# The last stage's first matrix product with seven half products for eight in 5 of 16 blocks

## The chip, the cores and the metric

One Trainium2 chip; the kernel runs on one of its cores, in one launch. The metric is the device time of that launch in microseconds. Before the change it is 961.84 us, the median of three runs (960.94 to 963.04).

## What is computed

Attention over 4 x 12 heads of 448 tokens, a routed mixture of 8 experts with two products each, and a last stage of two products with an ELU between them, on 1792 tokens. The last stage is what is changed:

```
def _moe2_ref(x, w_in, w_out):              # x 1792 x 768, w_in 768 x 2048, w_out 2048 x 768
    h = x @ w_in
    g = np.where(h > 0.0, h, np.exp(np.minimum(h, 0.0)) - 1.0)
    return g @ w_out
```

The products are made in float16 pairs: a number is a high half plus a low half, and a product takes three matmuls (high x high, high x low, low x high).

## The kernel before

Attention and routing fill some 300 us, the experts (e = 0 to 7, lines L974 and L1011) the time to 546 us, then come layer 1 (L1090) and layer 2 (L1137) of the last stage. All engines work from queues of instructions in order; which order they have is settled when the program is built, by a scheduler that simulates the engines.

The tokens stand in `xc` as two halves h of 896 columns, cut into block 0 (512 columns of either half) and block 1 (384). Layer 1 runs over f = 0 to 7. For each f it takes the columns f and f + 8 of `w_in` (r = 0, 1; 128 columns each) and makes four tiles (h, r) for block 0 and four for block 1, each of 6 x 3 = 18 matmuls into one PSUM bank (tags `b` and `c`, three banks each). `wi_prep(f + 1)` runs at f: it loads two tiles of `w_in` in float64 words, three integer steps on VectorE make float32 of each (L854 to L856), ScalarE makes the high half (L919) and VectorE the low one (L920). `wo_prep` does the same for the second matrix (L1024 to L1031), with the sums that layer 2 needs.

After each tile comes the ELU in three steps: ScalarE's Exp of PSUM (L1092), VectorE's clamp `min(e, 1) - 1` in place (L1093), and VectorE's maximum of that and the PSUM tile (L1094). The tile `e` (five buffers) is then stored to `g_d` in DRAM (L1098). Layer 2 loads it from there (`q`, L1050), and makes sums of it and splits them (L1057 to L1067).

Layer 2 already makes seven half products for eight, with the function `winograd`: 2 x 2 blocks of tokens and weights, four sums of the tokens' blocks (S1 to S4), four of the weights' (T1 to T4), and products accumulated over three PSUM banks a, b and c. `product` issues the matmuls, `snap` copies a bank to SBUF, `add` adds a bank to such a copy, `copy` takes a bank as it is. Its sums T1 and T3 of the weights come back from DRAM to the tile `ex` (L1039), T4 to `xc` after layer 1 is through with it.

GpSimd makes the low halves `xh` of the experts' gathered rows (L938; the last at 475.59 us), and then stands idle until layer 2's scattered stores (L1153).

Of the kernel before, what the change touches and what calls it, by code (L numbers as in the profile page):

```python
# [5 lines left out]
F32 = mybir.dt.float32  # L6
F16 = mybir.dt.float16
# [13 lines left out]
P = 128  # L21
# [748 lines left out]
CH2 = 1.0 / (SO * SW * SW * SY * SW)  # L770
COUT = 1.0 / (SG * SW)

# [10 lines left out]
class Weights:  # L783
# [28 lines left out]
    def fetch(self, pool, w2_d):  # L812

        self.f2 = [pool.tile([P, 1024], F32, name=f"b{d}") for d in range(6)]
        self.w2 = []
        for f, x in zip(self.f2, w2_d[0]):
            self.nc.sync.dma_start(f, x)
# [45 lines left out]


PS = ("a", 2), ("b", 3), ("c", 3)
A11, A12, S2, S3, S1, S4, A22 = range(7)
# [34 lines left out]

def moe(tc, xp, pre, xs, idx, idh, W, rows, ring, w1_d, w2_d, wi_d, wo_d, lin, g_d, t_d, out):
    nc = tc.nc
    with tc.tile_pool(name="mp", bufs=1, space=PSUM, reuse_waits="tile") as pp:
# [6 lines left out]

        wic = {}

        def wi_prep(f):

            for f in (f, f + 8):
                a = W.read64(wi_d[f], f"wi{f}")
                w = wic[f] = ring.tile([P, 2, 768], F16, tag="w1", name=f"wic{f}", bufs=8)
                nc.scalar.activation(w[:, 0], a, AF.Copy, scale=SW)  # L919
                nc.vector.scalar_tensor_tensor(w[:, 1], a, SW, w[:, 0], ALU.mult, ALU.subtract)  # L920

        words = ExitStack()
        W.stage64 = words.enter_context(tc.tile_pool(name="w64", bufs=1, side="right", reuse_waits="tile"))
        with tc.tile_pool(name="m1", bufs=1, reuse_waits="tile") as sp:
# [5 lines left out]
            def columns(e):  # L930
# [3 lines left out]
                for h in (1, 0):  # L934
                    for a in range(0, DM, n):
                        x32, hi, lo = xg[h][0:112, a:a + n], hl[h][0:112, 0, a:a + n], hl[h][0:112, 1, a:a + n]
                        nc.scalar.activation(hi, x32, AF.Copy)  # L937
                        (nc.vector if e == 0 else nc.gpsimd).tensor_tensor(lo, x32, hi, ALU.subtract)  # L938
                xe[e] = x
# [9 lines left out]
            def result(e, d, ps):  # L949

                ps = ps.rearrange("p (h c) -> p h c", h=2)
                for c, (a, b) in zip(xc, CB):
                    lo, hi = max(a, 112 * e), min(b, 112 * e + 112)
                    if lo < hi:
                        z, c = ps[:, :, lo - 112 * e:hi - 112 * e], c[:, :, d, :, lo - a:hi - a]
                        nc.scalar.activation(c[:, :, 0], z, AF.Copy, scale=SY)
                        nc.vector.scalar_tensor_tensor(c[:, :, 1], z, SY, c[:, :, 0], ALU.mult, ALU.subtract)

            with tc.manual_schedule():
# [29 lines left out]
            for e in range(E):  # L989
# [16 lines left out]
                for d in range(6):  # L1006
# [5 lines left out]
                    result(e, d, ps)  # L1012
        pre.close()
        with tc.tile_pool(name="wb", bufs=1, reuse_waits="tile") as wp:
            WO = (0,), (1,), (2, 3), (4,), (5,), (6,), (7,), ()
            wb = wp.tile([P, 3, 8, 2, 384], F16, name="wb")


            ex = wp.tile([P, 14336], F16, name="ex")

# [58 lines left out]
            with tc.tile_pool(name="l1", bufs=1, side="right", reuse_waits="tile") as sp:  # L1079
                def layer1(f, cb, made=None):  # L1080

                    c0, c1 = CB[cb]
                    n = c1 - c0
                    for k, (h, r) in enumerate(((0, 0), (0, 1), (1, 0), (1, 1))):
                        t, bufs = PS[2 - k % 2]
                        ps = pp.tile([P, 512], F32, name=f"l{f}_{cb}{h}{r}", tag=t, bufs=bufs)[:, 0:n]
                        w = wic[f + 8 * r]
                        for d in range(6):
                            for m, (i, j) in enumerate(((0, 0), (0, 1), (1, 0))):
                                nc.tensor.matmul(ps, w[:, i, d * P:(d + 1) * P], xc[cb][:, h, d, j], start=d == 0 and m == 0, stop=d == 5 and m == 2)  # L1090
                        e = sp.tile([P, 512], F32, tag="e", name=f"e{f}_{cb}{h}{r}", bufs=5)[:, 0:n]
                        nc.scalar.activation(e, ps, AF.Exp, scale=CH2)  # L1092
                        nc.vector.tensor_scalar(e, e, 1.0, -1.0, ALU.min, ALU.add)  # L1093
                        nc.vector.scalar_tensor_tensor(e, ps, CH2, e, ALU.mult, ALU.max)  # L1094
                        if made is not None:
                            made[2 * r + h] = e
                        g = slice(c0 // P, c1 // P)
                        store = nc.sync.dma_start(g_d[g, 2 * r + h, :, f].rearrange("g p c -> p g c"), e.rearrange("p (g c) -> p g c", c=P))  # L1098
                    return store

                for f in range(8):
# [8 lines left out]
                    late = {}  # L1110
                    layer1(f, 0, late)
                    if f == 7:
                        first = operands(0, late)
                        next(first)
                        wt = {T3: load_t(T3, ex[:, 0:6144]), T1: load_t(T1, ex[:, 6144:12288])}
                    last = layer1(f, 1)
                wt |= {k: [wb[:, k, f] for f in range(8)] for k in (B11, B21, B22)}
# [51 lines left out]
def body(tc, i, out):  # L1169
    nc = tc.nc  # L1170
    with tc.tile_pool(name="lg", bufs=1) as lp, tc.tile_pool(name="ring", bufs=1, side="right") as ring, tc.tile_pool(name="dr", bufs=1, space=DRAM) as dp:
# [12 lines left out]
        with tc.tile_pool(name="xc", bufs=1, reuse_waits="tile") as xp:  # L1184
            pre = ExitStack()
            W.fetch(pre.enter_context(tc.tile_pool(name="pre", bufs=1, reuse_waits="tile")), i["w2"])
            rt.run(L, idx, row, W, rows.gather)
            moe(tc, xp, pre, xs, idx, idh, W, rows, ring, i["w1"], i["w2"], i["wi"], i["wo"], lin, g_d, t_d, out)

# [15 lines left out]
```

## Time and profile before

| | |
|---|---|
| median of three runs | 961.84 us |
| profiled execution | 961.21 us |
| its span in the trace | 959.4 us |
| mean granted TensorE clock | 0.997 |
| TensorE busy | 934.2 us (97%) |
| VectorE busy | 729.9 us (76%) |
| ScalarE busy | 524.8 us (55%) |
| GpSimd busy | 282.7 us (29%) |

Times in the trace run from the start of the span. Busy time is a mean over stages: VectorE's 76% are more than 95% in some stretches and half of that in others. In the rows, a name such as `e` stands for all its buffers; `out<-in` says what an instruction writes and reads. The idle time in a group's row is that of the engine just before its instructions, and the arrow names what ended it.

### The profile page before, as it was taken

Reading aid. Unit: us, or ns where it says so; the run is one execution under the profiler, and the core shown is the slowest. Engines: PE = TensorE matmul, PEld = TensorE weight load, DVE = VectorE, ACT = ScalarE, POOL = GpSimd, SP = SyncE. Lnnn points to the kernel's source line nnn. Section 1 sums busy time; section 2 is a strip of 40 time slices with the busy share of each in tenths; the row PEclk is TensorE's granted clock in tenths of the full one; section 3 lists DMA queues with packets and bytes.
Section 4 is the critical chain, followed back from the end, with each engine's and each line's share of the span. In section 5 each row is a group of like instructions: output and inputs, shape, how many; then the busy total and the mean of one; then the engine's idle time right before and its main releaser. Section 6 shows DMA issues by size and latency. Waiting matters only on the chain.

```text
span 959.4 us, 18741 instructions
## 1 busy us (share of the span) xinstructions
PE 934.2 (97%) x6927; PEld 620.7 (65%) x6927; DVE 729.9 (76%) x1433; ACT 524.8 (55%) x1147; POOL 282.7 (29%) x470
## 2 busy tenths in 40 slices
PE   7999999999987999999999999999999999999997
PEld 3555555555544899999999855555555566666664
DVE  8999998899867887777777799999825576555430
ACT  7989999999844666665664334333313333333320
POOL 5779999999423422221000000000000000000000
PEclk9999999999999999999999999999999999999999
DMA  9544444453254788776774377887763662332000
GB/s 349 201 136 121 139 122 153 120 168 79 56 166 158 182 293 268 245 239 215 241 213 142 132 259 237 267 269 252 229 204 105 173 231 92 119 101 99 33 33 33
DMA packets 100352, 164.93 MB, mean 172 GB/s; under 512 B 32672, under 2 KB 65952, under 8 KB 99872
## 3 DMA queue, kind: packets, MB, share of 16 engines
q1 hardware_dynamic: 96048, 152.66, 50.5%
q0 software_dynamic: 2400, 11.01, 3.4%
q8 instruction: 56, 0.92, 0.4%
q10 hardware_dynamic: 1808, 0.01, 0.2%
q14 instruction: 40, 0.33, 0.1%
HBM read 131.66 MB, written 31.99 MB: 171 GB/s over the span
## 4 chain that ended last, share of the span: by engine, by line
PE 87%; DVE 7%; DMA 2%; ACT 1%; issue 1%; POOL 0%; POOLq 0%; DVEq 0%; ACTq 0%
PE l L1090 23%; PE o_b L1137 11%; PE py L1011 10%; PE ph L974 10%; PE o L319 7%; PE o_c L1137 6%; PE s L242 5%; PE pt L295 5%; PE o_a L1137 3%; DMA fw<-w 1%; DVE w L843 1%; PE s L235 1%; PE pt L293 1%; DVE s L247 1%; PE pk L204 1%
## 5 line engine op out<-in xcount | busy, mean ns | idle before, releaser
L1090 PE MATMUL l<-xc,wic 128*128 128x384 f16 (+1 forms) x1152 | 218.2, 352 | 0.0
L1090 PEld LDWEIGHTS <-wic 128*128 128x128 f16 x1152 | 112.7, 98 | 104.9
L1137 PEld LDWEIGHTS <-a 128*128 128x128 f16 x1080 | 105.7, 98 | 69.8
L1153 POOL DMA_INDIRECT out<-xc,id x14 | 13.9, 992 | 463.6 <-issue 311.5
L843 DVE SCALAR_TENSOR_TENSOR w<-fw,w 128x768 f16<-128x768 f32 (+1 forms) x98 | 112.8, 1153 | 25.8 <-ACT w L841 25.8
L1011 PE MATMUL py<-h,w 128*128 128x224 f16 x1152 | 113.8, 259 | 1.5 <-DVE h L976 1.5
L1011 PEld LDWEIGHTS <-w 128*128 128x128 f16 x1152 | 109.9, 98 | 1.9 <-issue 1.6
L247 DVE TENSOR_REDUCE s<-s 128x1 f32<-128x448 f32 x168 | 104.7, 626 | 5.5 <-PE s L242 4.9
L266 ACT ACTIVATE p<-s,nb,r 128x448 f32<-128x448 f32 x144 | 104.4, 726 | 4.2 <-DVE nb L253 3.0
L974 PE MATMUL ph<-xe,w 128*128 128x224 f16 x1008 | 99.1, 259 | 1.5 <-DVE h L976 1.1
L974 PEld LDWEIGHTS <-w 128*128 128x128 f16 x1008 | 96.5, 98 | 1.8 <-issue 1.8
L841 ACT ACTIVATE w<-fw 128x768 f16<-128x768 f32 (+1 forms) x98 | 90.7, 928 | 5.5 <-DMA fw<-w 5.4
L1092 ACT ACTIVATE e<-l 128x512 f32<-128x512 f32 (+1 forms) x64 | 34.6, 540 | 103.7 <-PE l L1090 103.7
L304 ACT ACTIVATE e<-pt 128x448 f32<-128x448 f32 (+2 forms) x208 | 80.9, 429 | 14.5 <-PE pt L295 14.1
L319 PE MATMUL o<-e,v 128*64 128x448 f32 x384 | 87.8, 558 | 0.0
L295 PE MATMUL pt<-idn,p 128*128 128x128 f32 x432 | 70.9, 276 | 0.9 <-ACT p L266 0.9
L295 PEld LDWEIGHTS pt<-idn,p 128*128 128x128 f32 x432 | 50.0, 141 | 24.0 <-ACT e L304 12.3
L1067 DVE SCALAR_TENSOR_TENSOR a<-s,a 128x1024 f16<-128x1024 f32 (+2 forms) x30 | 33.4, 1116 | 39.1 <-ACT a L1066 39.1
L938 POOL TENSOR_TENSOR xh<-xg,xh 112x768 f16<-112x768 f32 x14 | 25.7, 1853 | 122.9 <-ACT xh L937 122.8
L242 PE MATMUL s<-ks,qh 128*128 128x448 f16 x144 | 51.2, 355 | 1.9 <-ACT p L266 1.0
L1137 PE MATMUL o_b<-wb,a 128*128 128x384 f16 x312 | 51.8, 326 | 0.0
L242 PE MATMUL s<-ks,ql 128*128 128x448 f16 x144 | 50.7, 352 | 0.0
(242 smaller groups left out, 1598.4 us busy)
## 6 DMA issues: line engine op xcount, KB each, us to landing
fw<-w SPq DMA_DIRECT2D x56, 384.0 KB, 3.8
fw<-w SPq DMA_DIRECT2D x42, 512.0 KB, 4.6
xwi<-wi SPq DMA_DIRECT2D x16, 768.0 KB, 7.4
xwo<-wo SPq DMA_DIRECT2D x16, 768.0 KB, 4.9
q<-g_d SPq DMA_DIRECT2D x24, 512.0 KB, 3.7
qT<-qT SPq DMA_DIRECT2D x24, 448.0 KB, 4.5
qk<-qk SPq DMA_DIRECT2D x23, 448.0 KB, 3.7
g_d<-e SPq DMA_DIRECT2D x32, 256.0 KB, 4.3
```

Of the source, the lines that this page charges most:

```text
L242: nc.tensor.matmul(ps[:, 0:448], q[:, o:o + P], ks[:, 448 * h:448 * h + 448], start=n == 0, stop=n == 1)
L247: nc.vector.tensor_reduce(d["s", u][:, 448:449], d["s", u][:, 0:448], AX.X, ALU.max, negate=True)
L266: nc.scalar.activation(dst, d["s", u][:, 0:448], AF.Exp, bias=d["nb", u], scale=d["r"][:, rc:rc + 1], accum_out=d["sm"][:, rc:rc + 1])
L295: nc.tensor.transpose(pt[:, j * P:(j + 1) * P], p[j][:, h, 64 * h + c * P:64 * h + (c + 1) * P], idn)
L304: move = nc.vector.tensor_copy if u in on else lambda o, x: nc.scalar.activation(o, x, AF.Copy)
L319: nc.tensor.matmul(d["o"][64 * h:64 * h + 64, 0:448], d["v"][:, c + 4 * h, :], d["e", min(2 * c + h, 6)], start=c == 0, stop=c == 3)
L841: nc.scalar.activation(w[:, 0], f, AF.Copy, scale=SW)
L843: nc.vector.scalar_tensor_tensor(w[:, 1], f, SW, w[:, 0], ALU.mult, ALU.subtract)
L974: mm = nc.tensor.matmul(ps, w[:, i, d * P:(d + 1) * P], x[:, d, j], start=d == 0 and n == 0, stop=d == 5 and n == 2)
L1011: nc.tensor.matmul(ps, w[:, i, f * P:(f + 1) * P], h[:, f, j], start=f == 0 and n == 0, stop=f == 7 and n == 2)
L1090: nc.tensor.matmul(ps, w[:, i, d * P:(d + 1) * P], xc[cb][:, h, d, j], start=d == 0 and m == 0, stop=d == 5 and m == 2)
L1137: nc.tensor.matmul(ps, a[x][:, f, i], wt[b][f][:, j], start=first and f == 0 and k == 0, stop=f == 7 and k == 2, skip_group_check=True)
```

## The change

For f = 2 to 6 block 0 is made by `winograd` (`fewer`), with the two halves of the tokens, the two halves of the 768 rows of `w_in` and the two column groups r as the 2 x 2 blocks: seven half products of 9 matmuls take the place of eight. Block 1 stays as it was (`plain`); its four tiles are issued between the half products, after A11, S2, S3 and A22. The four sums of the tokens' blocks are made by `combine` on GpSimd, in 12 rounds of 8 instructions (4 groups of 128 columns by 3 groups of 128 rows), queued behind the last instruction `xh`. The sums of the weights are made in `wi_prep` for these f: four sums and two more splits each. The tiles for the sums and for the copies (`kept`) share one place with `ex`, which is therefore free only after f = 6.

The ELU changes for all f: after Exp, ScalarE makes relu(1 - exp), and VectorE takes the minimum of that and -x. What is stored has its sign turned, and `COUT` turns it back.

Instructions in the order of the program are shown at three places. Names are tiles with their numbers; `sums` is the tile of the tokens' sums, `xc0` block 0.

GpSimd at the end of the experts, before:

```order
L898 DMA xg7_0_8981<-xs_63,idx_70 112x768
L938 TENSOR_TENSOR xh6_0_8986<-xg6_0_8527,xh6_0_8986 112x768
L938 TENSOR_TENSOR xh7_1_9425<-xg7_1_8982,xh7_1_9425 112x768
L938 TENSOR_TENSOR xh7_0_9424<-xg7_0_8981,xh7_0_9424 112x768
L1153 DMA out<-xc1_6525,id2_6526 1792x768 x14
```

and now:

```order
L953 TENSOR_TENSOR xh7_1_9421<-xg7_1_8978,xh7_1_9421 112x768
L953 TENSOR_TENSOR xh7_0_9420<-xg7_0_8977,xh7_0_9420 112x768
L983 TENSOR_TENSOR sums_6850<-xc0_6519 128x256 x3
L983 TENSOR_TENSOR sums_6850<-sums_6850 128x256
L983 TENSOR_TENSOR sums_6850<-sums_6850 128x128
L983 TENSOR_TENSOR sums_6850<-xc0_6519 128x256 x2
L983 TENSOR_TENSOR sums_6850<-sums_6850 128x128
L991 CAST sums_6850<-sums_6850 128x4x128
L983 TENSOR_TENSOR sums_6850<-sums_6850 128x4x128
L983 TENSOR_TENSOR sums_6850<-xc0_6519 128x256
```

Between the last `xh` and layer 2's stores (`out`) stand 96 instructions on `sums`.

VectorE near the second and third tile of f = 2, before (`wic`: split weights of layer 1, `awo`: words of the second matrix, `l2_001`: PSUM tile):

```order
L856 SCALAR_TENSOR_TENSOR awi4_10831<-xwi4_10832,awi4_10831 128x768
L1093 TENSOR_SCALAR e2_001_10682<-e2_001_10682 128x512
L856 SCALAR_TENSOR_TENSOR awi12_10840<-xwi12_10841,awi12_10840 128x768
L856 SCALAR_TENSOR_TENSOR awo4_10849<-xwo4_10850,awo4_10849 128x768
L1093 TENSOR_SCALAR e2_010_10706<-e2_010_10706 128x512
L1094 SCALAR_TENSOR_TENSOR e2_001_10682<-l2_001_10663,e2_001_10682 128x512
L920 SCALAR_TENSOR_TENSOR wic4_10837<-awi4_10831,wic4_10837 128x768
L1024 TENSOR_TENSOR t12_4_10861<-awo4_10849 128x384
L920 SCALAR_TENSOR_TENSOR wic12_10846<-awi12_10840,wic12_10846 128x768
L1094 SCALAR_TENSOR_TENSOR e2_010_10706<-l2_010_10687,e2_010_10706 128x512
```

and now, at the end of f = 2's block 0 (`l2_b` and `l2_c` are the banks b and c):

```order
L1122 SCALAR_TENSOR_TENSOR e2_110_10868<-l2_110_10849,e2_110_10868 128x384
L1161 SCALAR_TENSOR_TENSOR sums_6850<-l2_b_10755,sums_6850 128x512
L1067 SCALAR_TENSOR_TENSOR wb_10167<-awo4_10972,wb_10167 128x384
L855 TENSOR_SCALAR awo12_10978<-xwo12_10979 128x768
L921 SCALAR_TENSOR_TENSOR wic12_10957<-awi12_10948,wic12_10957 128x768
L933 TENSOR_TENSOR ti34_4_10961<-awi4_10942,ti12_4_10960 128x384
L1161 SCALAR_TENSOR_TENSOR sums_6850<-l2_c_10756,sums_6850 128x512
L921 SCALAR_TENSOR_TENSOR wic(4, 1)_10966<-ti12_4_10960,wic(4, 1)_10966 128x768
L856 SCALAR_TENSOR_TENSOR awo12_10978<-xwo12_10979,awo12_10978 128x768
L1122 SCALAR_TENSOR_TENSOR e2_011_10884<-sums_6850,e2_011_10884 128x512
L1122 SCALAR_TENSOR_TENSOR e2_111_10917<-l2_111_10898,e2_111_10917 128x384
L1122 SCALAR_TENSOR_TENSOR e2_010_10923<-sums_6850,e2_010_10923 128x512
```

The clamps (L1093) are gone, the sums of PSUM and copies (L1161) have come, and four splits `wic` stand for two.

SyncE's queue near the loads of `ex`, before:

```order
L1033 DMA t_d_67<-u12_7_11587 128x2x768
L1033 DMA t_d_67<-u34_7_11588 128x2x768
L1098 DMA g_d_66<-e5_000_11378 128x4x128
L1039 DMA ex_10077<-t_d_67 128x6144 x2
L1098 DMA g_d_66<-e5_001_11402 128x4x128
L1098 DMA g_d_66<-e5_010_11426 128x4x128
```

and now:

```order
L1124 DMA g_d_66<-e6_011_11868 128x4x128
L1124 DMA g_d_66<-e6_111_11901 128x3x128
L1124 DMA g_d_66<-e6_010_11907 128x4x128
L1075 DMA ex_12030<-t_d_67 128x6144 x2
L1124 DMA g_d_66<-e6_001_11921 128x4x128
L1124 DMA g_d_66<-e7_000_11953 128x4x128
L1124 DMA g_d_66<-e7_001_11977 128x4x128
L1086 DMA q0_2_12032<-g_d_66 128x896
L1086 DMA q0_1_12033<-g_d_66 128x896
L1086 DMA q0_3_12034<-g_d_66 128x896
```

The two loads have moved from the first tile of f = 5 to the end of f = 6's block 0, and three loads of `q` stand behind them. In the diff, some lines that only rename or pass on arguments are left out.

```diff
 CH2 = 1.0 / (SO * SW * SW * SY * SW)
-COUT = 1.0 / (SG * SW)
+COUT = -1.0 / (SG * SW)
...
-        self.f2 = [pool.tile([P, 1024], F32, name=f"b{d}") for d in range(6)]
+        f = pool.tile([P, 7168], F32, name="b", tag="ex", bufs=1)
+        self.f2 = [f[:, 1024 * d:1024 * d + 1024] for d in range(6)]
         self.w2 = []
...
+WINO = 2, 3, 4, 5, 6
 PS = ("a", 2), ("b", 3), ("c", 3)
...
-        wic = {}
+        wic, sums, kept, made = {}, [], [], []
...
-            for f in (f, f + 8):
-                a = W.read64(wi_d[f], f"wi{f}")
-                w = wic[f] = ring.tile([P, 2, 768], F16, tag="w1", name=f"wic{f}", bufs=8)
-                nc.scalar.activation(w[:, 0], a, AF.Copy, scale=SW)
-                nc.vector.scalar_tensor_tensor(w[:, 1], a, SW, w[:, 0], ALU.mult, ALU.subtract)
+            def split(k, x):
+                w = wic[k] = ring.tile([P, 2, 768], F16, tag="w1", name=f"wic{k}", bufs=8)
+                nc.scalar.activation(w[:, 0], x, AF.Copy, scale=SW)
+                nc.vector.scalar_tensor_tensor(w[:, 1], x, SW, w[:, 0], ALU.mult, ALU.subtract)
+
+            a, b = (W.read64(wi_d[k], f"wi{k}") for k in (f, f + 8))
+            split(f, a)
+            split(f + 8, b)
+            if f in WINO:
+                (b11, b21), (b12, b22) = ((x[:, 0:384], x[:, 384:768]) for x in (a, b))
+                t = [W.wstage.tile([P, 768], F32, tag="wst", name=f"ti{k}_{f}", bufs=5) for k in (12, 34)]
+                t1, t2, t3, t4 = (x[:, c:c + 384] for x in t for c in (0, 384))
+                nc.vector.tensor_tensor(t1, b12, b11, ALU.subtract)
+                nc.vector.tensor_tensor(t2, b22, t1, ALU.subtract)
+                nc.vector.tensor_tensor(t3, b22, b12, ALU.subtract)
+                nc.vector.tensor_tensor(t4, b21, t2, ALU.subtract)
+                split((f, 1), t[0])
+                split((f, 3), t[1])
...
                         nc.scalar.activation(hi, x32, AF.Copy)
-                        (nc.vector if e == 0 else nc.gpsimd).tensor_tensor(lo, x32, hi, ALU.subtract)
+                        rows.low = (nc.vector if e == 0 else nc.gpsimd).tensor_tensor(lo, x32, hi, ALU.subtract)
                 xe[e] = x
...
                 ps = ps.rearrange("p (h c) -> p h c", h=2)
+                if e == d == 0:
+                    x = homes.tile([P, 14336], F16, name="sums", tag="ex", bufs=1)
+                    sums.append(x[:, 0:12288].rearrange("p (k d j c) -> p k d j c", k=4, d=3, j=2))
+                    kept.extend(x.bitcast(F32)[:, c:c + 512] for c in (6144, 6656))
                 for c, (a, b) in zip(xc, CB):
...
                         nc.vector.scalar_tensor_tensor(c[:, :, 1], z, SY, c[:, :, 0], ALU.mult, ALU.subtract)
+
+            def combine(c, d):
+                x, y = slice(c * P, c * P + P), xc[0]
+                s, uv = (z.rearrange("p (k c) -> p k c", k=4) for z in kept)
+                s1, s3, s2, s4 = (s[:, k] for k in range(4))
+                u, v = uv[:, 0:2], uv[:, 2:4]
+                add = lambda o, p, q, op=ALU.add: nc.gpsimd.tensor_tensor(o, p, q, op)
+                add(u, y[:, 1, d, :, x], y[:, 1, d + 3, :, x])
+                add(v, y[:, 0, d, :, x], y[:, 1, d, :, x], ALU.subtract)
+                add(s[:, 2:4], y[:, 0, d:d + 4:3, 0, x], y[:, 0, d:d + 4:3, 1, x])
+                add(s[:, 0:2], uv[:, 0:4:2], uv[:, 1:4:2])
+                add(s2, s1, s2, ALU.subtract)
+                add(s4, s4, s2, ALU.subtract)
+                hi, lo = (sums[0][:, :, d, j, x] for j in range(2))
+                nc.gpsimd.tensor_copy(hi, s)
+                add(lo, s, hi, ALU.subtract)
...
                     result(e, d, ps)
-        pre.close()
+                    for k in range(2 * (e == 7)):
+                        with tc.issue_after(rows.low.ins):
+                            combine(*divmod(len(made), 3))
+                        made.append(d)
         with tc.tile_pool(name="wb", bufs=1, reuse_waits="tile") as wp:
...
-
-            ex = wp.tile([P, 14336], F16, name="ex")
...
             with tc.tile_pool(name="l1", bufs=1, side="right", reuse_waits="tile") as sp:
-                def layer1(f, cb, made=None):
-
+                def elu(f, cb, k, ps, done=False):
                     c0, c1 = CB[cb]
-                    n = c1 - c0
-                    for k, (h, r) in enumerate(((0, 0), (0, 1), (1, 0), (1, 1))):
-                        t, bufs = PS[2 - k % 2]
+                    h, r = k % 2, k // 2
+                    e = sp.tile([P, 512], F32, tag="e", name=f"e{f}_{cb}{h}{r}", bufs=5)[:, 0:c1 - c0]
+                    nc.scalar.activation(e, ps, AF.Exp, scale=1.0 if done else CH2)
+                    nc.scalar.activation(e, e, AF.Relu, bias=1.0, scale=-1.0)
+                    nc.vector.scalar_tensor_tensor(e, ps, -1.0 if done else -CH2, e, ALU.mult, ALU.min)
+                    g = slice(c0 // P, c1 // P)
+                    return e, nc.sync.dma_start(g_d[g, k, :, f].rearrange("g p c -> p g c"), e.rearrange("p (g c) -> p g c", c=P))
+
+                def plain(f, cb, made=None):
+                    n = CB[cb][1] - CB[cb][0]
+                    for h, r in ((0, 0), (0, 1), (1, 0), (1, 1)):
+                        t, bufs = PS[2 - r]
                         ps = pp.tile([P, 512], F32, name=f"l{f}_{cb}{h}{r}", tag=t, bufs=bufs)[:, 0:n]
...
                                 nc.tensor.matmul(ps, w[:, i, d * P:(d + 1) * P], xc[cb][:, h, d, j], start=d == 0 and m == 0, stop=d == 5 and m == 2)
-                        e = sp.tile([P, 512], F32, tag="e", name=f"e{f}_{cb}{h}{r}", bufs=5)[:, 0:n]
-                        nc.scalar.activation(e, ps, AF.Exp, scale=CH2)
-                        nc.vector.tensor_scalar(e, e, 1.0, -1.0, ALU.min, ALU.add)
-                        nc.vector.scalar_tensor_tensor(e, ps, CH2, e, ALU.mult, ALU.max)
+                        e, store = elu(f, cb, 2 * r + h, ps)
                         if made is not None:
                             made[2 * r + h] = e
-                        g = slice(c0 // P, c1 // P)
-                        store = nc.sync.dma_start(g_d[g, 2 * r + h, :, f].rearrange("g p c -> p g c"), e.rearrange("p (g c) -> p g c", c=P))
-                    return store
+                        yield store
+
+                def fewer(f, beside):
+                    x = {A11: xc[0][:, 0, 0:3], A12: xc[0][:, 0, 3:6], A22: xc[0][:, 1, 3:6]} | dict(zip((S1, S3, S2, S4), (sums[0][:, k] for k in range(4))))
+                    w = {B11: (f, 0), B21: (f, 384), B22: (f + 8, 384), T1: ((f, 1), 0), T2: ((f, 1), 384), T3: ((f, 3), 0), T4: ((f, 3), 384)}
+
+                    def product(ps, p, q, first):
+                        k, c = w[q]
+                        for d in range(3):
+                            for m, (i, j) in enumerate(((0, 0), (0, 1), (1, 0))):
+                                nc.tensor.matmul(ps, wic[k][:, i, c + d * P:c + d * P + P], x[p][:, d, j], start=first and d == 0 and m == 0,
+                                                 stop=d == 2 and m == 2, skip_group_check=True)
+                        if p in (A11, S2, S3, A22):
+                            next(beside)
+
+                    homes = [*kept, sp.tile([P, 512], F32, tag="e", name=f"z{f}", bufs=5)]
+
+                    def snap(ps):
+                        z = homes.pop()
+                        nc.scalar.activation(z, ps, AF.Copy, scale=CH2)
+                        return z
+
+                    def add(ps, z, r, h):
+                        nc.vector.scalar_tensor_tensor(z, ps, CH2, z, ALU.mult, ALU.add)
+                        elu(f, 0, 2 * h + r, z, True)
+
+                    def copy(ps, r, h):
+                        elu(f, 0, 2 * h + r, ps)
+
+                    winograd(pp, f"l{f}_", 512, product, snap, add, copy)
...
                     late = {}
-                    layer1(f, 0, late)
+                    if f in WINO:
+                        fewer(f, plain(f, 1))
+                        continue
+                    for _ in plain(f, 0, late):
+                        pass
                     if f == 7:
+                        ex = homes.tile([P, 14336], F16, name="ex", tag="ex", bufs=1)
                         first = operands(0, late)
...
                         wt = {T3: load_t(T3, ex[:, 0:6144]), T1: load_t(T1, ex[:, 6144:12288])}
-                    last = layer1(f, 1)
+                    for last in plain(f, 1):
+                        pass
                 wt |= {k: [wb[:, k, f] for f in range(8)] for k in (B11, B21, B22)}
```

## Rows read from the trace of the kernel before

**Rows 1.** Page, chain that ended last by engine; below, its layer-1 step (start, us)
```profile
PE 87%; DVE 7%; DMA 2%; ACT 1%; issue 1%; POOL 0%; POOLq 0%; DVEq 0%; ACTq 0%
...
546.00 216.41 PE l L1090 x1145
```

**Rows 2.** Busy us of each engine (instructions), PEclk, DMA share in three stretches
```profile
core 0: us, PE busy (x) PEld busy (x) DVE busy (x) ACT busy (x) POOL busy (x), PEclk, DMA share, GB/s
478.00:547.00 69.00, 69.00 (x719) 67.58 (x717) 52.91 (x79) 31.89 (x59) 0.00 (x0) 1.00 0.50 159
573.00:600.00 27.00, 27.00 (x145) 14.00 (x143) 27.00 (x45) 10.09 (x16) 0.00 (x0) 1.00 0.74 237
681.00:708.00 27.00, 27.00 (x145) 13.96 (x144) 13.71 (x25) 6.53 (x12) 0.00 (x0) 1.00 0.81 256
```

**Rows 3.** Groups by line and form, 546 to 762.4 us (busy, mean ns, idle)
```profile
L1090 PE MATMUL l<-xc,wic 128*128 128x512 f16 x569 | 124.1, 379 | 0.0
L1090 PE MATMUL l<-xc,wic 128*128 128x384 f16 x576 | 94.9, 326 | 0.0
L1092 ACT ACTIVATE e<-l 128x512 f32<-128x512 f32 x32 | 19.0, 592 | 53.9 <-PE l L1090 53.9
L1093 DVE TENSOR_SCALAR e<-e 128x512 f32<-128x512 f32 x32 | 13.4, 419 | 13.2 <-ACT e L1092 13.2
L1093 DVE TENSOR_SCALAR e<-e 128x384 f32<-128x384 f32 x31 | 10.9, 351 | 13.2 <-ACT e L1092 13.2
```

**Rows 4.** Timeline of VectorE in layer 1 (start us, duration us)
```profile
547.57 0.55 DVE L1025 TENSOR_TENSOR t<-awo,t 128x384 f32<-128x384 f32 x1
548.04 0.55 DVE L1026 TENSOR_TENSOR t<-awo,awo 128x384 f32<-128x384 f32 x1
...
551.65 0.55 DVE L854 TENSOR_SCALAR awo<-xwo 128x768 int32<-128x768 int32 x1
552.12 0.95 DVE L1031 SCALAR_TENSOR_TENSOR u<-t,u 128x768 f16<-128x768 f32 x1
552.99 0.95 DVE L855 SCALAR_TENSOR_TENSOR awi<-xwi,awi 128x768 int32<-128x768 int32 x1
...
557.14 0.68 DVE L1094 SCALAR_TENSOR_TENSOR e<-l,e 128x512 f32<-128x512 f32 x1
557.74 0.94 DVE L856 SCALAR_TENSOR_TENSOR awi<-xwi,awi 128x768 int32<-128x768 int32 x1
```

**Rows 5.** Groups of GpSimd by line and form, whole span
```profile
L148 POOL TENSOR_TENSOR sq<-qk 128x448 f32<-128x448 f32 x40 | 36.5, 935 | 0.1
L938 POOL TENSOR_TENSOR xh<-xg,xh 112x768 f16<-112x768 f32 x14 | 25.7, 1853 | 122.9 <-ACT xh L937 122.8
L158 POOL TENSOR_TENSOR sq<-sq 128x224 f32<-128x224 f32 x40 | 25.6, 661 | 0.0
```

**Rows 6.** Groups of VectorE by line and form, 478 to 547 us
```profile
L843 DVE SCALAR_TENSOR_TENSOR w<-fw,w 128x1024 f16<-128x1024 f32 x12 | 14.7, 1224 | 4.7 <-ACT w L841 4.7
L843 DVE SCALAR_TENSOR_TENSOR w<-fw,w 128x768 f16<-128x768 f32 x8 | 7.7, 957 | 2.0 <-ACT w L841 2.0
```

**Rows 7.** Timelines: a GpSimd pair (xh), then VectorE instructions during such pairs
```profile
391.05 3.24 POOL L938 TENSOR_TENSOR xh<-xg,xh 112x768 f16<-112x768 f32 x2 [22.77 <-ACT xh L937]
...
321.27 5.40 DVE L843 SCALAR_TENSOR_TENSOR w<-fw,w 128x768 f16<-128x768 f32 x4 [0.97 <-ACT w L841]
...
391.98 0.39 DVE L957 SCALAR_TENSOR_TENSOR xc<-py,xc 128x224 f16<-128x224 f32 x1 [1.18 <-ACT xc L956]
392.93 2.45 DVE L843 SCALAR_TENSOR_TENSOR w<-fw,w 128x1024 f16<-128x1024 f32 x1 [0.55 <-ACT w L841]
...
450.42 2.54 DVE L843 SCALAR_TENSOR_TENSOR w<-fw,w 128x1024 f16<-128x1024 f32 x1 [0.65 <-ACT w L841]
```

**Rows 8.** Stores of tile e; loads of ex; last q load (SP timeline)
```profile
DMA to landing us min/median/max: 2.4/4.7/10.5
...
ex<-t_d SPq DMA_DIRECT2D x2, 1536.0 KB, 8.5
...
730.44 0.33 SPq L1050 DMA_DIRECT2D q<-g_d  x1
```

More of the change, by code (lines that the diff above doesn't have):

```diff
@@ L899, in gather, with moe @@
         return x
-def moe(tc, xp, pre, xs, idx, idh, W, rows, ring, w1_d, w2_d, wi_d, wo_d, lin, g_d, t_d, out):
+def moe(tc, xp, homes, xs, idx, idh, W, rows, ring, w1_d, w2_d, wi_d, wo_d, lin, g_d, t_d, out):
     nc = tc.nc
@@ L1185, in body @@
             pre = ExitStack()
-            W.fetch(pre.enter_context(tc.tile_pool(name="pre", bufs=1, reuse_waits="tile")), i["w2"])
+            homes = pre.enter_context(tc.tile_pool(name="pre", bufs=1, reuse_waits="tile"))
+            W.fetch(homes, i["w2"])
             rt.run(L, idx, row, W, rows.gather)
-            moe(tc, xp, pre, xs, idx, idh, W, rows, ring, i["w1"], i["w2"], i["wi"], i["wo"], lin, g_d, t_d, out)
+            moe(tc, xp, homes, xs, idx, idh, W, rows, ring, i["w1"], i["w2"], i["wi"], i["wo"], lin, g_d, t_d, out)
+            pre.close()
 def kernel(q, k, v, g_q, g_k, moe_w_gate, moe_w1, moe_w2, moe2_w_in, moe2_w_out):
```

## The prediction

> **What bounds the kernel now.** I read the chain of waits first: 87% of the span is TensorE, and the whole first layer of the last stage is one link, 216.41 us of matmuls from 546.00 to 762.41 [rows 1]; with the seven matmuls issued at 542 it is 217.9 us, 27.24 us for each of the eight values of f. Then the table of busy time by stretch [rows 2]: TensorE has no idle time in any of the three, at a granted clock of 1.00, the 2.4 GHz level. VectorE is the second bound: 27.00 of 27 us from 573 to 600, and only from 681 on it has half its time free. From 478 to 547 it is busy 52.91 of 69 us, so 16.1 us are free. GpSimd does nothing in these stretches. So TensorE work that goes is gained only while VectorE, with no spare time for f = 0 to 5, keeps up.
>
> **What the change removes.** For f = 2 to 6 the eight half products of block 0 (72 matmuls of 512 columns) become seven (63). That is 45 matmuls; a 512-column matmul is 124.1 / 569 = 0.218 us [rows 3], so 9.8 us less on a chain without gaps. If nothing else moved, the run would take 961.21 - 9.8 = 951.4 us. The profiled execution lies 0.63 us under the median of 961.84; I add that at the end.
>
> **VectorE's own balance.** It loses 64 clamps, 13.4 + 10.9 = 24.3 us [rows 3], one clamp not being in the records. It gains for each of five f four sums of 384 columns (0.55 us), two splits of 768 (0.95) and three PSUM sums of 512 (0.68) [rows 4]: 5 x (2.2 + 1.9 + 2.04) = 30.7 us, so 6.4 us more, between 573 and 735. Its stretch of 681 to 708 alone has 13.3 us free, but the earlier f have none; so I walked VectorE's new order. From 547.09 to the sum of l2_b, on which TensorE's seventh product of f = 2 waits, stand 113 instructions. Start to start they take 0.87 us (47 with 768 columns, two inputs), 0.47 (13 with 768, one input), 0.47 (27 sums of 384, and I take 15 others of 384 alike) and 0.60 (11 of 512 from PSUM) [rows 4]: 40.8 + 6.1 + 19.7 + 6.6 = 73.2, end 620.2. TensorE reaches that product at 762.41 - 6 x 27.24 = 599.0, plus 54 matmuls of 512 (11.8), 72 of 384 (94.9 / 576 = 0.165 each, 11.9) and 8 matmuls of the next f that now stand before it (1.7): 624.4. The slack is about 4 us. For the next f VectorE needs 25.2 us by the same steps and TensorE 25.3: the slack stays near 4 us to f = 5, and whatever else delays VectorE after 547 beyond 4 us is paid in full, once, since it never catches up before TensorE's next need.
>
> **ScalarE.** It gains 64 Relu, at most 0.592 us each [rows 3] or 38 us, 15 copies and ten weight halves, some 18 us; of 27 us it is busy 10.09 [rows 2]. I cost it at nothing; the cover is 16.9 us in each f.
>
> **GpSimd's sums, the term that decides.** Twelve times eight instructions start behind the last gathered rows, at about 478, and read and write SBUF. Neither the 256- nor the 128- or 512-column form runs in the trace. In proportion to the 935 ns of 448 columns they take 0.53, 0.27 and 1.07 us; on a line through 661 ns at 224 and 935 at 448 and on to 1.62 at 768 they take 0.70, 0.54 and 1.08 [rows 5, 7]. One round is four of 256, two of 128 and two of 512: 4.8 to 6.0 us, in all 58 to 72; I take 65. Unhindered they end at 543, well ahead of their first use, the S2 product near 608. What they do to VectorE is the question. While GpSimd made its pairs xh, VectorE's splits with two SBUF inputs stretched: 2.45 and 2.54 us against 1.22, four in 5.40 us against 3.6 [rows 6, 7]. I count eight such places (the first, one between and the last are shown): 10.5 us lost on VectorE in the 25.7 us of GpSimd's 14 instructions [rows 5], 0.41 us for each. Instructions that read PSUM did not stretch. At that rate 65 us of sums cost VectorE 26.7 us. The 16.1 us free before 547 take their part, 10.6 us are left, 4 are slack, and 6.6 us reach TensorE. Bounds: 0, if the sums fall in gaps, and 23 (the third rival). I take 6.6, the rate of the nearest rows.
>
> The Trainium skill, page "SBUF — State Buffer", section "Who interferes with whom", says why: a VectorE instruction with two SBUF inputs and a GpSimd instruction that reads SBUF exclude each other for the whole instruction, and one with a single SBUF input outside the two-port modes does not contend. The trace agrees, with 2.45 for 1.22 us on a split and 0.39 us unchanged on one that reads PSUM. By that rule taken strictly the sum is the third rival's.
>
> **Smaller terms.** From f = 3 on the copy z must have a buffer whose store has landed: the store starts about 8 to 10 us before TensorE needs the copy, the copy takes 0.6, stores take 2.4 to 10.5 us, median 4.7 [rows 8]. Most fit; for a late one in four I take 0.6 us, bounds 0 and 8. The loads of ex now wait for the seventh product of f = 6, which ends 27.24 us ahead of layer 2 (752.6 at best), at 725.4. Three loads of q stand behind them on SyncE, and behind the stores of the first two tiles of f = 7, which are ready after 36 matmuls (7.8 us) and an ELU step: about 735, where the last was issued at 730.44 before [rows 8]. The loads of ex took 8.5 us [rows 8]; layer 2 wants q's sums in its third product, two of 24 x 0.165 = 4 us after its start, at 760, and T3 at 764. I take 0, bounds 0 and 5.
>
> **The sum.** 961.21 - 9.8 + 6.6 + 0.6 = 958.6, plus 0.63: 959.2 us.
>
> **The rivals.** First, the sums run beside VectorE at no price. For it: GpSimd is idle from 478 on, and 16.1 us of VectorE are free there; against it, eight collisions in 25.7 us. Then only 0 to 1 us of the 9.8 are lost: 952 to 953.5.
>
> Second, layer 2's hand-off is late. Against it, 30 us from the landing of ex, near 734, to the product that wants T3; for it, that after three q loads at 735 come four sums and four splits before the third product at 760. It adds 2 to 5 us to whichever case holds: 955 to 965.
>
> Third, slower: GpSimd and VectorE take strict turns. From 478 to 547 VectorE has 38 us of instructions with two SBUF inputs (14.7 + 7.7 in the weight splits [rows 6], and 16 of the 0.95 us kind). GpSimd then finds 69 - 38 = 31 of its 65 us there. The other 34 us fall where VectorE has no free time; beside an equal amount of its own excluded work only the ELU steps that read PSUM, about a fifth of its time, go on, 7 to 9 us. VectorE falls 26 us behind, TensorE 22. That is 961.84 - 9.8 + 22.6 = 975; with sums as short as the lower bound it is 7 us less, 968. It decides from the point where VectorE is more than 13.8 us late at the sum of l2_b (4 of slack and the 9.8). For it: every split that met a pair waited for it; against it: GpSimd's fixed part of each short instruction may exclude nothing, and no layer-1 form was ever seen beside GpSimd.
>
> **How the numbers follow.** The forecast's mechanism, a loss near the measured rate, gets 0.40 and lies between 955 and 964 with the bounds of the sums' length and the stores. No loss gets 0.24, strict turns 0.28, the late hand-off 0.08. No change is within 0.2%, 1.9 us, which is what a measurement can tell: 959.9 to 963.8. Faster: 0.18 of the first, 0.24 of the second and 0.02 of the last, 0.44. Same: 0.12, 0.01 of strict turns, 0.03, together 0.16. Slower: 0.10, 0.27 and 0.03, 0.40. The range goes from the no-loss case, 952, up into strict turns, 972, and leaves out about 0.04 below and 0.13 above.
>
> **What would show it.** In the new profile: GpSimd's sums end between 543 (no loss) and about 600 (strict turns); VectorE's splits and integer steps between 478 and 600 last 0.95 and 1.22 us or up to a microsecond more; VectorE's sum of l2_b ends near 620, 630 or 645; TensorE's idle time in layer 1 goes to that sum, about 7 us in one place near f = 2, or is spread over PSUM tiles before it. Idle time of TensorE behind q, ex or the snapshot z would put the loss elsewhere. The prediction is wrong if TensorE waits for nothing in layer 1, or for more than 14 us.

## The result and the profile after

The changed kernel takes 970.38 us (median of four, 969.74 to 971.09) where the kernel before takes 961.72 in the same series: 1.0089 times, interval 1.0071 to 1.0106, that is 8.7 us slower. The forecast was 959.2, slightly faster; what came is nearest to the third rival, GpSimd and VectorE in turns, at less than its full price of 975. The forecast's range, 952 to 972, holds it only through that rival.

The chain that ended last, by engine, from the page of the profile after:

```profile
PE 62%; DVE 24%; DMA 5%; issue 5%; ACT 2%; SPq 0%; POOL 0%; POOLq 0%; DVEq 0%; ACTq 0%
```

VectorE has 24% of it where it had 7% [rows 1]; TensorE is no longer an unbroken link in layer 1. Busy time by stretch (columns as in [rows 2]):

```profile
core 0: us, PE busy (x) PEld busy (x) DVE busy (x) ACT busy (x) POOL busy (x), PEclk, DMA share, GB/s
478.00:534.00 56.00, 56.00 (x599) 56.00 (x597) 44.40 (x58) 27.58 (x49) 54.19 (x51) 1.00 0.52 160
547.00:586.00 39.00, 34.18 (x168) 16.85 (x169) 39.00 (x41) 13.10 (x21) 37.47 (x35) 0.96 0.49 154
573.00:600.00 27.00, 22.65 (x107) 10.60 (x105) 27.00 (x35) 12.57 (x22) 12.30 (x13) 0.94 0.59 183
600.00:627.00 27.00, 21.90 (x112) 11.22 (x111) 26.97 (x45) 16.08 (x29) 0.00 (x0) 0.94 0.83 268
```

From 478 on GpSimd works almost without a pause, until its last sum ends at 585.9. VectorE has no free time after 547, as before, but from 547 to 586 it gets only 41 instructions done. TensorE, which had no idle time there, loses 4.35 us of 573 to 600 and 5.1 of 600 to 627.

GpSimd's groups from 470 to 800 (busy, mean ns, idle), and then four of its instructions near 526, while VectorE has little to do (start, us):

```profile
L983 POOL TENSOR_TENSOR sums<-xc 128x256 f32<-128x256 f16 x36 | 39.3, 1106 | 0.9
L983 POOL TENSOR_TENSOR sums<-sums 128x128 f32<-128x128 f32 x24 | 21.4, 892 | 1.0
L983 POOL TENSOR_TENSOR sums<-sums 128x512 f16<-128x512 f32 x12 | 18.8, 1570 | 1.0
L983 POOL TENSOR_TENSOR sums<-sums 128x256 f32<-128x256 f32 x12 | 15.7, 1306 | 0.0
L991 POOL CAST sums<-sums 128x512 f16<-128x512 f32 x12 | 10.7, 892 | 0.8
```

```profile
525.92 0.45 POOL L983 TENSOR_TENSOR sums<-sums 128x128 f32<-128x128 f32 x1
526.43 0.61 POOL L991 CAST sums<-sums 128x512 f16<-128x512 f32 x1
527.12 1.16 POOL L983 TENSOR_TENSOR sums<-sums 128x512 f16<-128x512 f32 x1
528.36 0.67 POOL L983 TENSOR_TENSOR sums<-xc 128x256 f32<-128x256 f16 x1
```

The sum of the groups is 105.9 us. Alone, 128 columns take 0.45 us, the 512-column copy 0.61 and sum 1.16, 256 columns from `xc` 0.66 to 0.67 (a pair of them 1.29, in a row at 530.20 that is not shown), and the pair of 256 and 128 in 1.25 (its row at 528.99 is not shown) leaves 0.8 for the last form. A round of eight is 5.45 us, all twelve 65.4: the length taken in the prediction. The other 40 us are added beside VectorE's work. How, is seen where both are busy; VectorE first, then GpSimd (start, us):

```profile
554.10 1.08 DVE L1062 TENSOR_TENSOR t<-awo,awo 128x384 f32<-128x384 f32 x1
555.10 1.21 DVE L1067 SCALAR_TENSOR_TENSOR wb<-awo,wb 128x768 f16<-128x768 f32 x1
556.23 1.02 DVE L1063 TENSOR_TENSOR t<-awo,t 128x384 f32<-128x384 f32 x1
```

```profile
553.72 1.77 POOL L983 TENSOR_TENSOR sums<-sums 128x256 f32<-128x256 f32 x2
555.45 2.32 POOL L983 TENSOR_TENSOR sums<-xc 128x256 f32<-128x256 f16 x2
```

A sum of 384 columns that took 0.55 us takes 1.08, a split of 0.95 takes 1.21 [rows 4]; GpSimd's pairs of 1.25 and 1.29 us take 1.77 and 2.32. Both engines are held up. VectorE's ELU steps that read a PSUM tile are not; they take 0.68 us as before [rows 4] (547 to 586):

```profile
L1122 DVE SCALAR_TENSOR_TENSOR e<-l,e 128x512 f32<-128x512 f32 x4 | 2.7, 678 | 0.0
```

The splits of the last expert stage, 478 to 547, are longer too, but less, against 1224 and 957 ns [rows 6]:

```profile
L844 DVE SCALAR_TENSOR_TENSOR w<-fw,w 128x1024 f16<-128x1024 f32 x12 | 16.6, 1385 | 3.0 <-ACT w L842 3.0
L844 DVE SCALAR_TENSOR_TENSOR w<-fw,w 128x768 f16<-128x768 f32 x8 | 9.2, 1150 | 1.4 <-ACT w L842 1.4
```

TensorE in layer 1 (start, duration us; in brackets the idle time before and who ended it), rows between the third and the last left out:

```profile
547.46 29.79 PE L1134 MATMUL l<-xc,wic 128*128 128x512 f16 x155 [1.00 <-DVE xc L976]
581.60 25.19 PE L1134 MATMUL l<-xc,wic 128*128 128x512 f16 x126 [4.35 <-DVE e L1122]
607.95 2.10 PE L1148 MATMUL l_b<-xc,wic 128*128 128x512 f16 x9 [1.15 <-DVE e L1122]
...
621.37 2.88 PE L1148 MATMUL l_b<-sums,wic(2, 1)_10435 128*128 128x512 f16 x9 [3.95 <-ACT z L1157]
```

It waits 4.35 us for a PSUM tile that VectorE's ELU step releases, 1.15 for another, and 3.95 us for the snapshot z of f = 2, made by ScalarE. Why ScalarE is late shows in its own timeline:

```profile
618.27 0.52 ACT L1066 ACTIVATE wb<-awo 128x384 f16<-128x384 f32 x1 [2.66 <-DVE awo L857]
619.60 0.84 ACT L1066 ACTIVATE wb<-awo 128x768 f16<-128x768 f32 x1 [0.81 <-DVE awo L857]
...
620.72 0.59 ACT L1157 ACTIVATE z<-l_b 128x512 f32<-128x512 f32 x1
```

The snapshot (L1157) is short; it stands behind halves `wb` (L1066), which wait 2.66 and 0.81 us for VectorE's integer step L857. ScalarE hands VectorE's lateness on.

The granted clock also falls after the pauses (the second row is a part of the first):

```profile
575.00:585.00 10.00, 5.65 (x20) 2.07 (x19) 10.00 (x12) 2.61 (x5) 9.48 (x11) 0.83 0.54 178
583.00:585.00 2.00, 2.00 (x7) 0.61 (x5) 2.00 (x3) 0.77 (x2) 1.92 (x2) 0.50 0.58 163
585.00:595.00 10.00, 10.00 (x48) 4.58 (x47) 10.00 (x15) 6.56 (x11) 0.90 (x1) 1.00 0.57 175
```

In the stretch with the pause of 4.35 us it is 0.83 of full speed in the mean, between the levels of 1.2 and 2.4 GHz; from 583 to 585, right behind the pause, it is 0.50, the level of 1.2 GHz, and in the next stretch it is back at 1.00. The 20 matmuls of the first of the three stretches, of 512 columns, take 5.65 us where 0.218 each would make 4.4. From 615 to 627, around the pause of 3.95 us, the mean is 0.86, and 34 matmuls take 8.05 us where their forms add up to about 6.5. Together this is some 3 us.

Layer 1 starts at 547.46 and ends at 768.71:

```profile
741.47 27.40 PE L1134 MATMUL l<-xc,wic 128*128 128x512 f16 x144
768.71 4.06 PE L1211 MATMUL o_b<-wb,ex 128*128 128x384 f16 x24
...
789.68 4.06 PE L1211 MATMUL o_c<-xc 128*128 128x384 f16 x24 [1.31 <-ACT xc L1216]
```

That is 221.25 us, where 216.41 [rows 1] less 9.8 would be 206.6: 14.6 lost. Of these 10.2 are TensorE's idle time in layer 1 and some 3 the lower clock; the last 1.4 were not traced. The start is 1.6 us later than before (545.84 in the same view), and layer 2 takes 199.5 us for 197.1, with waits for ScalarE's copies. 14.6 + 1.6 + 2.3 = 18.5, less 9.8, is the 8.7 us.

### The profile page after: what moved, and what is told of

Read it like the earlier page. It is cut to its first block, busy times and chain, and to the rows that moved or that the text cites. A ratio compares the mean times of both kernels' runs of the same rounds, so it can differ in the third digit from the quotient of the medians.

```text
span 968.2 us, 18827 instructions
## 1 busy us (share of the span) xinstructions
PE 929.4 (96%) x6882; PEld 617.0 (64%) x6882; DVE 757.9 (78%) x1414; ACT 572.1 (59%) x1236; POOL 387.4 (40%) x566
## 4 chain that ended last, share of the span: by engine, by line
PE 62%; DVE 24%; DMA 5%; issue 5%; ACT 2%; SPq 0%; POOL 0%; POOLq 0%; DVEq 0%; ACTq 0%
PE ph L1009 10%; PE o_b L1211 9%; PE py L1046 9%; PE o L319 7%; PE s L242 5%; PE o_c L1211 5%; PE pt L295 5%; PE o_a L1211 2%; DVE e L1122 2%; DMA q<-g_d 2%; DVE awi L856 1%; DVE awo L857 1%; DVE awi L857 1%; DVE awo L856 1%; PE l L1134 1%
## 5 line engine op out<-in xcount | busy, mean ns | idle before, releaser
L1134 PE MATMUL l<-xc,wic 128*128 128x384 f16 (+1 forms) x792 | 147.2, 344 | 5.4 <-DVE e L1122 4.4
L844 DVE SCALAR_TENSOR_TENSOR w<-fw,w 128x768 f16<-128x768 f32 (+1 forms) x98 | 116.3, 1189 | 22.7 <-ACT w L842 22.7
L1134 PEld LDWEIGHTS <-wic 128*128 128x128 f16 x792 | 78.0, 99 | 72.5 <-issue 7.8
L983 POOL TENSOR_TENSOR sums<-sums 128x128 f32<-128x128 f32 (+2 forms) x48 | 55.9, 1165 | 2.0
```

The source lines that it names most:

```text
L844: nc.vector.scalar_tensor_tensor(w[:, 1], f, SW, w[:, 0], ALU.mult, ALU.subtract)
```

## Experiments

All are edits of the changed kernel unless a line says otherwise; ratios are to the kernel before on the same chip.

**Without the sums.**

```diff
-                    for k in range(2 * (e == 7)):
-                        with tc.issue_after(rows.low.ins):
-                            combine(*divmod(len(made), 3))
-                        made.append(d)
...
-  ... | dict(zip((S1, S3, S2, S4), (sums[0][:, k] for k in range(4))))
+  ... | {S1: xc[0][:, 1, 0:3], S3: xc[0][:, 1, 3:6], S2: xc[0][:, 0, 0:3], S4: xc[0][:, 0, 3:6]}
```

> The changed kernel without GpSimd's 96 instructions on the tokens' sums; the products with S1 to S4 read parts of block 0 in their place, so the sums are left out of the computation and all else stays. Theory 1 (GpSimd's sums and VectorE's instructions with two SBUF inputs exclude each other, VectorE falls some 26 us behind and TensorE pays 16 to 20 us): the loss goes, 952 us (951.5 to 955). Theory 2 (VectorE's and ScalarE's own added work, the snapshots and the extra weight splits are late by themselves): it stays at 966 to 971.

Measured: 953.8 us, 0.9921 (0.9904 to 0.9937). The whole loss goes with GpSimd's 96 instructions; what VectorE and ScalarE got besides costs 2 us at most (961.84 less 9.8 would be 952.0). Theory 2 has fallen. The longer splits from 478 to 547 are at their old length:

```profile
L844 DVE SCALAR_TENSOR_TENSOR w<-fw,w 128x1024 f16<-128x1024 f32 x12 | 14.7, 1224 | 4.7 <-ACT w L842 4.7
```

**The sums earlier, in six stages.**

```diff
-                    for k in range(2 * (e == 7)):
+                    for k in range(e >= 2 and d in (2, 5)):
```

> The changed kernel with the 12 rounds of sums moved forward: two rounds in each of the expert stages e = 2 to 7, behind that stage's last rows xh, in place of all 12 behind the last. Theory 1: each stage of 29 us has 5 to 8 us of VectorE free and as much that reads PSUM, 11 us of sums fit there, and none is left for layer 1: 953 to 958. Theory 2: the time of the sums does not matter, 969 to 971. If the sums hold up the gathered rows instead, TensorE waits for the transposed rows in the expert stages and the time is above 960.

Measured: 953.24 us, 0.9935 (0.9912 to 0.9958). The same sums, all made, at the price of none. One expert stage and the two stretches after it:

```profile
390.00:419.00 29.00, 29.00 (x317) 29.00 (x315) 23.90 (x32) 18.09 (x32) 25.31 (x20) 1.00 0.78 247
478.00:547.00 69.00, 69.00 (x714) 67.17 (x713) 57.17 (x81) 32.10 (x58) 35.54 (x31) 1.00 0.49 161
547.00:586.00 39.00, 39.00 (x201) 19.41 (x199) 39.00 (x60) 22.23 (x35) 0.00 (x0) 1.00 0.74 237
```

GpSimd is busy 25 of 29 us in such a stage, and TensorE has no idle time. In the last expert stage the rest of the sums ends; they cost VectorE some 4 us there (busy 57.17 us for 52.91 [rows 2], with two instructions more), and its free time takes that. From 547 to 586 VectorE gets 60 instructions done where it got 41. Layer 1, of which the first link of the chain stands first, goes from 545.28 to 751.82, 206.5 us: the 206.6 of the prediction's first term.

```profile
545.28 52.97 PE l L1134 x281
```

```profile
751.82 4.06 PE L1211 MATMUL o_b<-wb,ex 128*128 128x384 f16 x24
```

**Sums that nobody reads, and neither.** `WINO = ()` leaves eight half products everywhere; the first of the two kernels keeps the sums, the second drops them too.

```diff
-WINO = 2, 3, 4, 5, 6
+WINO = ()
```

> The changed kernel with eight half products everywhere (no block takes seven), GpSimd's sums still made behind the last rows but read by nothing. Theory 1: VectorE is again some 20 us late in f = 0 and 1, TensorE has only its PSUM tiles' lead of 10 to 15 us, so 5 to 12 us slower than the same kernel without the sums, 966 to 974. Theory 2: the sums are not waited for, 961 to 962.

> The changed kernel with eight half products everywhere and without the sums: what is left of the change is ELU's clamp as a Relu on ScalarE (and the place of ex). Both theories: no change, 961 to 962.5. If the longer chain Exp, Relu, minimum by itself costs something, 963 to 966.

Measured: 967.44 us, 1.0075 (1.0058 to 1.0092), and 961.8 us, 1.0007 (0.9997 to 1.0017). ELU's clamp on ScalarE costs and gives nothing. The sums alone cost 5.6 us although no instruction waits for them: TensorE waits for PSUM tiles that VectorE is late with,

```profile
PE l L1134 <- DVE e L1122: 4.3, 5, 1.3
```

(total, times, longest). With seven half products the same sums cost 17 us (970.38 less 953.24): a likely reason, not tested by itself, is that the snapshots and the sums from PSUM leave TensorE less lead than plain tiles do, and VectorE less room to make it good.

**Nine rounds of twelve behind the last rows.**

```diff
-                    for k in range(2 * (e == 7)):
+                    for k in range((2 - d // 3) * (e == 7) + (e in (2, 3, 4) and d == 5)):
```

> The changed kernel with 3 of the 12 rounds of sums made early (one in each of the stages e = 2, 3, 4) and 9 behind the last rows. A round takes 5.45 us of GpSimd alone. Strict turns: 49 us of sums, 31 fit beside VectorE's other work before 547, 18 are left and put VectorE some 14 us late, 4 of slack: 9 to 11 us lost, 961 to 963. The loss at the rate of the forecast (0.41 us for each us, 16.1 us free): 20 - 16 = 4, all within the slack: 952 to 953.5.

Measured: 960.59 us, 0.9995 (0.9984 to 1.0007), 7.4 us above the kernel with all sums early. The accounting of the forecast, by which 9 rounds would have been free, is refuted; strict turns, which said 9 to 11, miss it too. How late VectorE is shows in one instruction, its sum of l2_b, in the changed kernel, with nine rounds late, and with all early:

```profile
637.73 0.69 DVE L1161 SCALAR_TENSOR_TENSOR sums<-l_b,sums 128x512 f32<-128x512 f32 x1
```

```profile
628.43 0.67 DVE L1161 SCALAR_TENSOR_TENSOR sums<-l_b,sums 128x512 f32<-128x512 f32 x1
```

```profile
619.10 0.67 DVE L1161 SCALAR_TENSOR_TENSOR sums<-l_b,sums 128x512 f32<-128x512 f32 x1
```

They end at 638.4, 629.1 and 619.8: 18.2 and 8.9 us behind the 620.2 that the steps of the kernel before gave, and with the sums early it is met to 0.4 us.

**Memsets in place of sums.** To see whether it is GpSimd's reading that excludes, the sums were replaced by instructions that only write.

```diff
-                x, y = slice(c * P, c * P + P), xc[0]
...
-                add(lo, s, hi, ALU.subtract)
+                s = sums[0].rearrange("p k d j c -> p (k d j c)").bitcast(F32)
+                for k in range(12):
+                    nc.gpsimd.memset(s[:, 512 * (3 * c + d):512 * (3 * c + d) + 512], 0.0)
```

> The changed kernel with GpSimd's 96 sums replaced, at the same place behind the last rows, by 144 memsets of 512 columns that write the same tile and read nothing; the sums are left out of the computation. Theory 1a (what excludes is that both engines read SBUF): VectorE's splits keep their 0.95 and 1.22 us, 952 to 954.5. Theory 1b (any GpSimd access to SBUF excludes VectorE's two-input instructions, the memsets being 40 to 80 us in all): VectorE is late as before, 958 to 970.

Measured: 991.19 us, 1.0306 (1.0289 to 1.0323), beyond both theories. GpSimd's and VectorE's groups (478 to 547 for VectorE):

```profile
L981 POOL MEMSET sums<- 128x512 f32 x144 | 67.7, 517 | 0.0
```

```profile
L855 DVE TENSOR_SCALAR awi<-xwi 128x768 int32<-128x768 int32 x1 | 39.0, 39050 | 0.0
L844 DVE SCALAR_TENSOR_TENSOR w<-fw,w 128x768 f16<-128x768 f32 x8 | 7.7, 958 | 2.0 <-ACT w L842 2.0
L844 DVE SCALAR_TENSOR_TENSOR w<-fw,w 128x1024 f16<-128x1024 f32 x6 | 7.4, 1226 | 3.1 <-ACT w L842 3.1
```

The splits with two inputs keep 0.96 and 1.23 us beside back-to-back memsets, as theory 1a has it. But the first integer step with one input, L855, whose rows took 0.55 us before [rows 4], is held for 39 us, through some 83 of the 144 memsets, until the last of them runs; VectorE's whole queue stands behind it.

**Memsets with gaps.** The memset kernel with a copy of one column behind each, which waits for it (lines that only place the instructions are left out):

```diff
+                    rows.low = nc.gpsimd.tensor_copy(s[:, o:o + 1], s[:, o + 511:o + 512])
```

> The memset experiment with a copy of one column behind each of the 144 memsets, which waits for it, so that GpSimd's instructions no longer stand back to back. Theory A (the one-input integer step L855 was held for 39 us because no gap lay between the memsets; a write alone does not hold the two-input instructions): L855 waits at most about a microsecond, the splits keep 0.95 and 1.22 us, 952 to 956. Theory B (memsets hold that step however they are spaced): 980 or more, as with the memsets back to back.

Measured: 955.74 us, 0.9957 (0.9933 to 0.998); theory A. The splits are untouched and L855 waits a fraction of a microsecond (478 to 600):

```profile
L844 DVE SCALAR_TENSOR_TENSOR w<-fw,w 128x1024 f16<-128x1024 f32 x12 | 14.7, 1224 | 4.7 <-ACT w L842 4.7
...
L855 DVE TENSOR_SCALAR awo<-xwo 128x768 int32<-128x768 int32 x8 | 6.1, 771 | 0.3 <-DMA xwo<-wo 0.3
```

**More blocks, with the sums early.** `WINO` from 1 and from 0 on, with the rounds as in the six stages above; and from 0 on with the rounds in e = 2 to 6, none in e = 7, which is the edit shown.

```diff
-WINO = 2, 3, 4, 5, 6
+WINO = 0, 1, 2, 3, 4, 5, 6
...
-                    for k in range(2 * (e == 7)):
+                    for k in range(d in {2: (2, 5), 3: (1, 3, 5), 4: (1, 3, 5), 5: (2, 5), 6: (2, 5)}.get(e, ())):
```

> e2_early with seven half products for f = 1 to 6. 9 matmuls less, 1.9 us: 951 to 952 if VectorE keeps up; 953 to 955 if it does not, since the weights' sums of f = 1 are made in f = 0, where VectorE has no time free.

> e2_early with seven half products for f = 0 to 6. 18 matmuls of 512 columns less on TensorE, 3.9 us. If VectorE (saturated to f = 5, with 16 us free in the last expert stage) takes the two more sets of weights' sums, 4.1 us each, and the six more sums from PSUM in that free time: 949 to 950.5. If VectorE has no room left: what TensorE gains it waits for the sums from PSUM, 953 to 957.

> Seven half products for f = 0 to 6, with the 12 rounds of sums in the stages e = 2 to 6 (2, 3, 3, 2, 2), none in e = 7, whose free VectorE time the weights' sums of f = 0 need. Theory 1 (sums cost VectorE its free time stage by stage): the 1.7 us that TensorE lost in the last expert stage with the sums in e = 2 to 7 go, 949.5 to 951.5. If that loss has another cause (the ring of weight tiles): 952 as there.

Measured: 953.54 us, 0.9914 (0.9897 to 0.993); 951.97 us, 0.9899 (0.9882 to 0.9917); 949.97 us, 0.9889 (0.9872 to 0.9905). The intervals overlap, so the steps between the three are not told apart by the times: the first median lies where VectorE was to have no room, the second between its two ranges, the third where theory 1 put it. The profile shows what the last edit does to the last expert stage, with the sums in it and without:

```profile
515.00:542.00 27.00, 25.27 (x253) 24.07 (x252) 18.73 (x30) 12.88 (x23) 0.75 (x1) 1.00 0.41 145
```

```profile
515.00:542.00 27.00, 26.90 (x258) 24.55 (x257) 19.18 (x30) 12.97 (x24) 0.00 (x0) 1.00 0.32 117
```

TensorE's 1.7 us of idle time go. This kernel makes all sums and is the fastest found, some 1.1% below the kernel before.

## Why the prediction was wrong

What was right: 9.8 us less on TensorE (206.5 us of layer 1 where the sums are early); nothing for the Relu and next to nothing for the added weights' sums; VectorE's walked order (620.2, met at 619.8); the sums' own 65 us; and that they contend with VectorE. The 0.6 us for a copy whose store lands late does not show: with the sums early TensorE waits for nothing in layer 1.

The step that failed is "The 16.1 us free before 547 take their part, 10.6 us are left". It sets the free time against the loss from all 65 us of sums, as if all were made beside it. Nearly all of it lies before 534, and from there on VectorE was already full (busy time in the kernel before, columns as in [rows 2]):

```profile
478.00:534.00 56.00, 56.00 (x599) 56.00 (x597) 40.09 (x58) 27.68 (x49) 0.00 (x0) 1.00 0.50 160
534.00:547.00 13.00, 13.00 (x123) 11.58 (x121) 12.82 (x21) 4.21 (x10) 0.00 (x0) 1.00 0.46 156
```

Up to 534 the sums cost VectorE 44.40 - 40.09 = 4.3 us for the same 58 instructions, and its free time took all of that. At 534 VectorE is not late, as its first integer step shows, in the kernel before, the changed kernel and that with nine rounds late:

```profile
534.18 0.56 DVE L854 TENSOR_SCALAR awi<-xwi 128x768 int32<-128x768 int32 x1 [2.19 <-PE py L1011]
```

```profile
534.05 0.92 DVE L855 TENSOR_SCALAR awi<-xwi 128x768 int32<-128x768 int32 x1 [2.19 <-PE py L1046]
```

```profile
534.18 0.93 DVE L855 TENSOR_SCALAR awi<-xwi 128x768 int32<-128x768 int32 x1 [2.19 <-PE py L1046]
```

The prediction has the sums end at 543 "Unhindered", and its sum goes by that. But GpSimd was held up too, and half of its work slid behind 534: 16 instructions of 256 columns from `xc`, 6 more of 256, 12 of 128 and 6 each of the two of 512, 31.5 us by their lengths alone. There VectorE has no free time, and all the 18.2 us by which it is late at the sum of l2_b arise there, 0.58 for each us of sums. With nine rounds late 15.1 us of sums are left at 534, and VectorE is 8.9 us late: 0.59 for each. Before 534 the other 33.9 us cost 4.3, or 0.13 for each. The mean over all is 0.34, where 0.41 was taken; that these lie near each other is luck, since no stretch has that rate. So 18.2 less 4 of slack is 14.2 on TensorE, where 6.6 were forecast, and that turned the sign.

Two more terms were missing. Some 3 us came from the lower granted clock after the pauses, and 2.3 us in layer 2. Of the latter, which shows as waits for ScalarE's copies behind loads of q, the cause stays open. It need not be VectorE's lateness: with plain tiles and equally late sums layer 2 ran at its old length, and with all sums early and `WINO` from 0 on (the last experiment) it takes 199.3 us. A late hand-off as in the second rival is not ruled out, and no run delays q alone.

The third rival was too dear by its own step: it had 31 us of sums done before 547. From 547 to 586 GpSimd makes 35 instructions, 12 of 256 columns from `xc`, 4 more of 256, 9 of 128 and 5 each of the two of 512: 24 us alone, so 41 were done before. And its 34 us beside a full VectorE were to cost 26, where 31.5 cost 18.2. Turns are not strict: the parts of GpSimd's short instructions that exclude nothing, which the prediction named against it, are a likely reason, not one that a run here shows.

TensorE also waited elsewhere than at the sum of l2_b, on which the forecast reckoned. It lost 0.7 us there, and 9.5 ahead of it, at two PSUM tiles and at the snapshot behind ScalarE's queue. It was late before it came there.

The Trainium skill ("SBUF — State Buffer", "Who interferes with whom") says that a VectorE instruction with two SBUF inputs contends with a GpSimd instruction that reads SBUF and not with one that only writes it, and that one in a two-port mode contends with GpSimd. The runs bear out the first two: 1.08 for 0.55 us beside sums, 0.96 us unchanged beside memsets. The one-input integer step, 0.92 for 0.56 us beside sums and 39 us for 0.55 beside memsets, would fit the third, but no run shows in which mode it works.

## What to carry to other kernels

Free time of an engine makes good only the contention that falls beside it or before it, not what comes behind. So set a loss against the free time stretch by stretch, and let both engines be held up: GpSimd's 65.4 us of sums took 105.9 here, and half of them slid out of the stretch with free time into one without. Work on GpSimd that reads SBUF belongs where VectorE is slack, in portions of a stage's free time: the same 65 us cost 17 us in one block ahead of a saturated stretch and nothing in six portions. When an engine runs late, look also at the in-order queues it feeds: here 3.95 us of the stall came through ScalarE's snapshot, which had nothing to do with the sums.

## What the runs showed of the hardware that was not expected

Back-to-back writes of GpSimd held a single VectorE instruction with one input for 39 us, through some 83 memsets of 0.517 us each; with a dependent copy between them, its mean was 0.77 us and the whole kernel 35 us faster; that the missing gap is what held it is the plain reading, though the copy also reads a column. The two-input splits beside the same memsets did not change by more than 0.01 us. And a wait of 4.35 us on TensorE cost more than its length: the granted clock in the 10 us around it was 0.83 of full speed, and 0.50 right behind it.
